# Three chained matrix products in seven block products: y over the whole contraction, with a stored third matrix of seven forms

## The chip, the cores and the metric

One NeuronCore of a Trainium2 chip. The metric is device time in microseconds of one execution. Engines: TensorE (PE; its weight loads PEld), VectorE (DVE), ScalarE (ACT), GpSimd (POOL) and SyncE (SP), which only issues DMAs. Each engine works through its own instructions in order.

## The reference, cut to what matters

Attention (4 batches, 12 heads, 448 positions, head width 64, with a mix over heads ahead of the softmax and one behind it) gives x of 1792 tokens x 768. Then

```
a = x @ w1;  b = x @ w2            # 768 -> 1024
h = a * b @ w3                     # 1024 -> 1024
x2 = h @ w_out                     # 1024 -> 768, called y in the kernel
h2 = max(x2 @ w_in, 0);  out = h2 * h2 @ w_out2     # 768 -> 2048 -> 768
```

All in float32. There is nothing between w3 and w_out, so the kernel multiplies these two once (p34, 1024 x 768) and computes y = (a * b) @ p34.

## The kernel before, in words

A float32 matrix is split into a high part (a copy rounded by ACT) and a low part (the rest, subtracted by DVE or POOL), and a product is three matmuls: high x high, high x low, low x high (`mm3`). The 1792 tokens are two halves of 896, a half is two tiles t of 448 columns. Matrices are kept transposed: a chunk is 128 rows of features x 448 tokens.

After the attention the work is a list of units, and each unit a few pieces of weights. One piece after another, `stage` issues for each engine, in an order fixed in the code: loads for the piece seven ahead (SP), the high part four ahead (ACT, `high`, L122), the low part three ahead (POOL, `rest`, L164), then functions that earlier pieces left in `late`, then the piece's own matmuls and reads (`go`). In this document a slot is the time of one piece.

Units in order, for the first half: l1 (a and b for 8 row blocks of 128), with w_out's pieces between them; p34 (8 units, 3 pieces each: w3 and w_out to p34, stored by ACT in `w34d`); the l1 units of row blocks 6 and 7; ly (y, 6 units); l3 products (named qh00 to qh07 in the trace, 7 block products of two halves each, from four products of halves of x2 and w_in); l4. During p34 and ly, `side` packs w_in for later (ACT fold L95, DVE L1116 and L1117, store). For the second half: l1 as block products (q00 to q31), ly, l3 and l4 as block products.

ly before: unit n is the block of 128 rows n of y; in 3 pieces of 3, 3 and 2 chunks of the contraction, for t = 0 and 1, PE multiplies with ab of this half. ab is stored split: `l1` and `l1_quad` multiply a and b in the PSUM bank (L789, L922), and `split_late` then makes the high (ACT, L771) and low part (DVE, L772). When a block is done, `yquad` reads it. The l3 product that follows wants seven forms of y: with B11, B12, B21, B22 for (half of the rows, t), B11, T1 = B12 - B11, T2 = B22 - T1, B22, T3 = B22 - B12, B21 and T4 = B21 - T2, each as high and low. `yquad` works per pair of row blocks j, as the blocks come.

`wl` and `wh` are ten buffers each, weight pieces of `ly` come into four `raw` buffers. PSUM has eight banks (`m`).

Of the kernel before, what the change touches and what calls it, by code (L numbers as in the profile page):

```python
# [9 lines left out]
F = mybir.dt.float32  # L10
# [28 lines left out]
def fused_kernel(ctx, tc, q, k, v, w_pre, w_post, w1, w2, w3t, wo, win, wo2, eye, out):  # L39
# [15 lines left out]
    def f32(ap):  # L55
        return ap.bitcast(F)
# [10 lines left out]
    class Weights:  # L67
# [480 lines left out]


    class Moe:  # L550
        def __init__(self, pre):
# [4 lines left out]
            self.sides, self.step = {}, 0  # L556
            self.hq = {}
            for hf in range(2):
                if hf == 0:
                    l1 = [self.l1(hf, m, s) for m in range(6) for s in range(2)]  # L560
                else:
                    l1 = [self.l1_quad(j, s) for j in range(4) for s in range(2)]
                if hf == 0:

                    wop = [self.wo_piece(c, h) for c in range(8) for h in range(2)]
                    mixed, rest = l1[:4] + wop[:6], wop[6:]
                    for i in range(8):
                        mixed.append(l1[4 + i])
                        for _ in range(1 + (i % 4 == 3)):
# [9 lines left out]
                self.units += [self.ly(hf, n) for n in range(6)]  # L579
                if hf == 0:  # L580
                    k = self.turned
                    self.free = {(i, t) for i in (*range(self.p34_at, k - 4), *range(k, k + 4)) for t in (0, 1)}
                    self.free |= {(i, 1) for i in range(k - 4, k)}
                    self.free |= {(k + 9 + e, 0) for e in range(6)}
                    self.free |= {(k + 17, 0)}
# [12 lines left out]
            for u in range(self.turned, len(self.units)):  # L598
                n, quad = len(self.units[u][0]), self.pieces[self.at[u]][0] is None
                for i in range(n if quad else 0):  # L600
                    self.lead[self.at[u] + i] = (4 if i < 6 else 3 if i < 8 else i > 9) if n > 7 else 2 if u > self.turned + 6 else 1
            self.keep = {
                self.at[i] + j: u[0][:, u[1] * j : u[1] * j + u[1]]
                for i, u in enumerate(kept) if u for j in range(len(self.units[i][0]))
            }

        def place(self, wp):
# [98 lines left out]
        def run(self, ps):  # L706
# [71 lines left out]
        def l1(self, hf, m, second):  # L778
            def run(ws, t, acc=None):
# [129 lines left out]
        def l1_quad(self, j, second):  # L909
            def done(r, t, acc, x=None, y=None):  # L910
                m = 2 * j + r
                if not second:
# [5 lines left out]
                    return  # L918
                ab = self.xy["ab", 1, m, t] = self.pair(f"ab1_{m}_{t}")
                if y is not None:  # L920
                    self.add(acc, x, y)
                nc.vector.tensor_tensor(acc, acc, self.xy["a", m, t], ALU.mult)  # L922
                self.split_late(ab, acc)

            src = [w12d[int(second), 2 * j + r] for r in range(2)]
            return self.quad(f"{j}{int(second)}", src, lambda: self.xq, 3, done)
# [88 lines left out]

        def yquad(self, hf, n, t, acc):
            j, kh = divmod(n, 2)
            if n == 0 and t == hf:
                xy = [self.new_xy(f"y{hf}_{t}", t) for t in range(2)]
                self.yq = {}  # L1020
                for c in range(3):
                    for name, u, o in (("B11", 0, 0), ("B21", 0, 3), ("T1", 1, 0), ("B22", 1, 3)):
                        self.yq[name, c] = tuple(x[:, o + c] for x in xy[u])
                    for name in ("T2", "T3", "T4"):
                        self.yq[name, c] = self.pair(f"y{hf}{name}{c}")
            b = self.yq
            V, G = nc.vector, nc.gpsimd

            def raw(name):
                b[name, j, "raw"] = self.tile(f"y{hf}{name}raw{j}")  # L1030
                return b[name, j, "raw"]

            def lo(name, x, eng=V):
                h, l = b[name, j]
                eng.tensor_tensor(l, x, f32(h), ALU.subtract)

            def hi(name, x):
                nc.scalar.activation(b[name, j][0], x, AF.Copy)

            def diff(name, x, y):  # L1040
                V.tensor_tensor(raw(name), x, y, ALU.subtract)

            name = f"B{kh + 1}{t + 1}"
            r = lambda n: b[n, j, "raw"]
            if name == "B22":
                diff("T2", acc, r("T1"))
                diff("T3", acc, r("B12"))
                hi("T2", r("T2"))
                hi("B22", acc)
                lo("T2", r("T2"))  # L1050
                lo("B22", acc)

                def rest():
                    for x in ("T3", "T4"):
                        hi(x, r(x))
                    for x in ("T3", "T4"):
                        lo(x, r(x), G if j < 2 else V)

                self.late[0].append(lambda: diff("T4", r("B21"), r("T2")))
                self.late[1].append(rest)  # L1060
                return
            nc.scalar.activation(raw(name), acc, AF.Copy)
            if name != "B12":
                hi(name, r(name))
                lo(name, r(name), G)
            if kh == 0 and all((n, j, "raw") in b for n in ("B11", "B12")):
                diff("T1", r("B12"), r("B11"))
                hi("T1", r("T1"))
                lo("T1", r("T1"), G)

        def wo_piece(self, c, h):
# [3 lines left out]
        def p34(self, m):  # L1075
            acc = {}

            def run(ws, i):
                for t in range(2):
# [4 lines left out]
                    if i < 2:  # L1084
                        continue
                    o = self.tile(f"o34_{m}_{t}")[:, :HC]
                    nc.scalar.activation(o, acc[t], AF.Copy)
                    nc.scalar.dma_start(
                        w34d[3 * t : 3 * t + 3, :, m].rearrange("n p c -> p n c"), o.rearrange("p (n c) -> p n c", c=128)
                    )  # L1090

            return [(w3t[m, :, HC * i : min(HC * i + HC, 1024)], True) for i in range(3)], run

        def ly(self, hf, n):
            acc = {}

            def run(ws, i):
                for t in (1, 0) if hf and n == 0 else (0, 1):
                    if i == 0:
                        acc[t] = self.psum(f"y{hf}_{n}_{t}")  # L1100
                    cs = range(3 * i, min(3 * i + 3, 8))
                    mm3(acc[t], [(self.chunk(ws, c), self.xy["ab", hf, c, t]) for c in cs], i == 0, i == 2)
                    if i == 2:
                        self.yquad(hf, n, t, acc[t])

            src = w34d[n].rearrange("p c n -> p (c n)")
            return [(src[:, HC * i : min(HC * i + HC, 1024)], False) for i in range(3)], run

# [215 lines left out]
```

## Time and profile before

| | us |
|---|---|
| median of 3 runs (1263.72 to 1266.94) | 1265.95 |
| the profiled execution, its own time | 1266.82 |
| its span, first to last instruction | 1265.0 |
| PE, DVE, ACT, POOL busy | 1238.2, 912.4, 776.7, 601.3 |

The page's parts are shares over the whole span. The chain of waits goes back from the last instruction: PE has 86% of it. The table of the queues gives q1 (SP's) 49.1% of 16 DMA engines and q10 (ACT's) 5.2%. What a change in one stage is worth is read from the rows of that stage.

### The profile page before, as it was taken

How to read it: one execution, taken by the hardware profiler on the slowest of the kernel's cores; microseconds unless marked ns; L12 is line 12 of the kernel's file. 1: busy time of each engine (PE TensorE's matmuls, PEld its weight loads, DVE VectorE, ACT ScalarE, POOL GpSimd, SP SyncE). 2: the span in 40 equal slices, each digit the busy share in tenths (PEclk: the TensorE clock that was granted, in tenths of full speed). 3: DMA queues.
4: the chain of work that ended last, by engine and by line, in shares of the span. 5: the costliest groups of instructions: out<-in, count | busy, mean ns of one | idle time of the engine just before them, and what ended most of it. 6: DMA issues, size and time to landing. Idle time of an engine off the chain costs nothing.

```text
span 1265.0 us, 24184 instructions
## 1 busy us (share of the span) xinstructions
PE 1238.2 (98%) x8326; PEld 1069.9 (85%) x8326; DVE 912.4 (72%) x1746; ACT 776.7 (61%) x1786; POOL 601.3 (48%) x707
## 2 busy tenths in 40 slices
PE   7999999999999899999999999999999999999998
PEld 3677777776776698999999999999999999999998
DVE  4888889889887967766455767579767424766967
ACT  5988888888987755555444756455433344653543
POOL 4354346246321313333356544444765464846756
PEclk9999999999999999999999999999999999999999
DMA  6666466565646657799654676466521116145042
GB/s 216 172 176 201 133 192 221 135 172 177 204 127 209 207 151 230 219 295 335 198 177 140 201 244 200 169 223 212 183 70 51 56 57 194 51 137 176 30 152 88
DMA packets 135696, 214.47 MB, mean 170 GB/s; under 512 B 24981, under 2 KB 104341, under 8 KB 135061
## 3 DMA queue, kind: packets, MB, share of 16 engines
q1 hardware_dynamic: 111696, 190.29, 49.1%
q10 hardware_dynamic: 23877, 22.63, 5.2%
q8 instruction: 66, 1.08, 0.4%
q14 instruction: 57, 0.47, 0.1%
HBM read 128.73 MB, written 45.61 MB: 138 GB/s over the span
## 4 chain that ended last, share of the span: by engine, by line
PE 86%; DVE 4%; DMA 3%; ACT 3%; issue 2%; POOL 2%; SPq 0%; ACTq 0%; POOLq 0%; DVEq 0%
PE l L62 16%; PE y L62 9%; PE sp L338 8%; PE tp L403 5%; PE p L62 5%; PE pv L455 5%; PE sc L312 4%; DMA r<-s 2%; PE e L62 1%; DVE pl L394 1%; DMA kraw<-k 1%; ACT p L352 1%; DVE nm L344 1%; ACT ph L378 1%; DVE p L417 1%
## 5 line engine op out<-in xcount | busy, mean ns | idle before, releaser
L164 POOL TENSOR_TENSOR wl<-f,wh 128x256 fp32r<-128x256 f32 (+1 forms) x104 | 96.9, 932 | 189.3 <-ACT wh L122 149.9
L338 PE MATMUL sp<-r,kpre 120*120 120x448 f32 x360 | 158.8, 561 | 11.6 <-ACT p L352 6.7
L352 ACT ACTIVATE p<-sp,nm 120x448 f32<-120x448 f32 x180 | 113.9, 644 | 49.9 <-DVE nm L344 49.3
L344 DVE TENSOR_REDUCE nm<-sp 120x1 f32<-120x448 f32 x180 | 107.4, 617 | 42.2 <-PE sp L338 37.9
L394 DVE SCALAR_TENSOR_TENSOR pl<-p,sm,ph 120x448 f16<-120x448 f32 (+3 forms) x270 | 131.8, 541 | 0.3 <-POOL ph L380 0.3
L367 POOL TENSOR_SCALAR sm<-sm 120x2 f32<-120x2 f32 (+3 forms) x94 | 24.5, 261 | 214.8 <-ACT p L352 210.7
L403 PEld LDWEIGHTS <-ph 120*128 120x128 f16 x1260 | 93.0, 98 | 29.8 <-issue 23.1
L378 ACT ACTIVATE ph<-p,sm 120x448 f16<-120x448 f32 (+1 forms) x180 | 107.9, 666 | 12.8 <-DVE sm L372 11.7
L403 PE MATMUL tp<-kwh,ph 120*128 120x120 f16 x630 | 106.0, 217 | 3.0 <-ACT p L415 2.1
L338 PEld LDWEIGHTS sp<-r,kpre 120*120 120x120 f32 x360 | 58.5, 183 | 55.8 <-issue 19.3
L403 PE MATMUL tp<-kwh,pl 120*128 120x120 f16 x630 | 105.1, 216 | 0.0
L403 PE MATMUL tp<-kwl,ph 120*128 120x120 f16 x630 | 105.1, 216 | 0.0
L312 PE MATMUL sc<-kt,qh 128*110 128x448 f32 (+1 forms) x192 | 98.3, 512 | 2.2 <-DVE kt L276 1.5
L323 ACT ACTIVATE s<-sc 110x448 f32<-110x448 f32 (+1 forms) x186 | 90.8, 562 | 6.3 <-PE sc L312 5.3
L122 ACT ACTIVATE wh<-f 128x256 fp32r<-128x256 f32 (+1 forms) x104 | 48.1, 463 | 57.5 <-DVE f L108 50.5
L164 POOL TENSOR_TENSOR wl<-quadh,wh 128x384 fp32r<-128x384 f32 x48 | 51.4, 1075 | 66.9 <-ACT wh L122 54.5
L455 PE MATMUL pv<-p,v 128*64 128x110 f32 (+1 forms) x1536 | 81.0, 262 | 0.6 <-ACT xs L465 0.6
L95 ACT ACTIVATE y<-raw 128x384 f32<-128x384 f32 (+1 forms) x120 | 59.0, 494 | 30.3 <-DMA raw<-wo 16.5
L455 PEld LDWEIGHTS pv<-p,v 128*64 128x64 f32 x1536 | 74.1, 137 | 4.1 <-ACT xs L465 0.9
L108 DVE SCALAR_TENSOR_TENSOR f<-raw,f 128x384 int32<-128x384 int32 (+1 forms) x120 | 71.9, 599 | 4.1
L417 DVE TENSOR_SCALAR p<-tp,iv 128x360 f32<-128x360 f32 x132 | 72.6, 577 | 2.1 <-PE tp L403 2.1
L312 PE MATMUL sc<-kt,ql 128*110 128x448 f32 (+1 forms) x192 | 70.8, 369 | 0.0
(3094 smaller groups left out, 3907.7 us busy)
## 6 DMA issues: line engine op xcount, KB each, us to landing
r<-s SPq DMA_DIRECT2D x172, 210.0 KB
raw<-w SPq DMA_DIRECT2D x32, 384.0 KB
sraw<-win SPq DMA_DIRECT2D x32, 384.0 KB
raw<-wo SPq DMA_DIRECT2D x48, 256.0 KB
kraw<-k SPq DMA_DIRECT2D x24, 448.0 KB
quadh<-wind SPq DMA_DIRECT2D x24, 384.0 KB
qraw<-q SPq DMA_DIRECT2D x35, 220.0 KB
v<-v SPq DMA_DIRECT2D x4, 1536.0 KB
```

The costliest lines, as they stand in the source:

```text
L62: nc.tensor.matmul(acc, w, x, start=(first and i == 0 and j == 0), stop=(last and i == n - 1 and j == 2), skip_group_check=again,)
L164: eng.tensor_tensor(self.out[i][1], self.ft.pop(i), f32(self.out[i][0]), ALU.subtract)
L312: nc.tensor.matmul(sc[:ic], t[:, hh * ic : hh * ic + ic], self.kt[b, h // 2][:, h % 2], start=(i == 0), stop=(i == 1))
L323: nc.scalar.activation(self.st[n][:ic, h], self.sc.pop((n, h))[:ic], AF.Copy)
L338: nc.tensor.matmul(t[:kk], self.kpre[:kk, :kk], self.rt.pop(g)[:kk], start=True, stop=True)
L344: nc.vector.tensor_reduce(nm[:kk], self.sp[g][:kk], AX.X, ALU.max, negate=True)
L352: nc.scalar.activation(p[:kk], self.sp.pop(g)[:kk], AF.Exp, bias=self.nm.pop(g)[:kk], accum_out=self.sm[g // 2][:kk, g % 2 : g % 2 + 1],)
L378: nc.scalar.activation(h[:, to], p[:, fr], AF.Copy, scale=sm)
L394: nc.vector.scalar_tensor_tensor(l[:, to], p[:, fr], sm, h[:, to], ALU.mult, ALU.subtract)
L403: nc.tensor.matmul(t[:, j], p[:, at : at + 128], w, start=(i == 0), stop=(i == 2))
L417: nc.vector.tensor_scalar(d, t[:, main], self.iv, None, ALU.mult)
L455: nc.tensor.matmul(t[64 * e : 64 * e + 64, x, :w], self.v[b][:, j, g], self.p2[n][:, j * NH + g, :w], start=(j == 0), stop=(j == JC - 1),)
```

## The change

The seven block products that l1 and l3 already use are now used for y as well, over the whole contraction: ab is cut into two halves of the rows (contraction) and two tiles, y likewise, p34 into four blocks.

- p34 is stored as seven forms of 512 x 384, `w7d[7, 4, 128, 384]`: three blocks as they come (ACT's DMA queue) and four sums or differences, made by DVE one slot later and stored by SP two slots later.
- ly has 7 units, one for each product, of 4 pieces (chunks c). In a piece, PE multiplies the 384 columns of the weight form with one chunk of the ab form: three pairs p of 128 columns, in three PSUM banks, nine matmuls. Products of even number add up in banks X, those of odd number in Z, and a bank is read four slots after it was begun or continued (`yread`).
- ab is kept unrounded in SBUF. The seven forms of it are made per chunk: a difference on DVE for T1 to T4, the high part on ACT, the low part on DVE (even c) or POOL (odd c). `plan_forms` fixes the slots: difference 12 (first half) or 14 (second), high 10 and low 9 pieces ahead, or as soon as the inputs are there.
- `yread` copies or adds the banks and makes the same seven forms of y, all of them in the last three units.
- Pieces of `ly` come into the six `quad` buffers. The side work runs in p34 and in all l1 units of row blocks 6 and 7, and in one slot of each of the first four ly units. The order of w_in's rows is the plain one.

```diff
-    w34d = dram.tile([6, 128, 8, 128], F, name="w34d")
+    w7d = dram.tile([7, 4, 128, DM // 2], F, name="w7d")
...
-                t = self.pre.tile([128, WT], F, tag="raw", name=f"raw{i}", bufs=self.nraw)
+                t = self.ap.tile([128, PW], F, tag="quad", name=f"raw{i}", bufs=6)
...
+    LY_FORMS = ("B11", "T1", "T2", "B22", "T3", "B21", "T4")
+    FORM_OF = {"T1": ("B12", "B11"), "T2": ("B22", "T1"), "T3": ("B22", "B12"), "T4": ("B21", "T2")}
+    LEAD0, LEAD1 = (12, 10, 9), (14, 10, 9)
...
-                    self.free = {(i, t) for i in (*range(self.p34_at, k - 4), *range(k, k + 4)) for t in (0, 1)}
-                    self.free |= {(i, 1) for i in range(k - 4, k)}
+                    self.free = {(i, t) for i in range(self.p34_at, k) for t in (0, 1)}
+                    self.free |= {(i, 1) for i in range(k, k + 4)}
...
+            lead = (LEAD0, LEAD1)[hf]
+            for s, n in enumerate(LY_FORMS):
+                for c in range(4):
+                    u = 4 * s + c
+                    if n[0] == "T":
+                        p = max([at(u - lead[0])] + [ready[x, c] for x in FORM_OF[n]])
+                        ready[n, c] = put(p, self.form_diff, n, c) + 1
+                    p = put(max(at(u - lead[1]), ready[n, c]), self.form_hi, n, c)
+                    p = put(max(at(u - lead[2]), p + 1), self.form_lo, n, c)
...
+        def form_hi(self, hf, n, c):
+            self.fp[hf, n, c] = self.pair(f"ab{hf}{n}{c}")
+            nc.scalar.activation(self.fp[hf, n, c][0], self.raws[hf, n, c], AF.Copy)
+
+        def form_lo(self, hf, n, c):
+            h, l = self.fp[hf, n, c]
+            (nc.gpsimd if c % 2 else nc.vector).tensor_tensor(l, self.raws[hf, n, c], f32(h), ALU.subtract)
...
                 def go():
+                    for f, *a in self.todo.pop(p, []):
+                        f(*a)
...
-                    ab = self.xy["ab", hf, m, t] = self.pair(f"ab{hf}_{m}_{t}")
-                    nc.vector.tensor_tensor(acc, acc, self.xy["a", m, t], ALU.mult)
-                    self.split_late(ab, acc)
+                    ab = self.raws[hf, f"B{m // 4 + 1}{t + 1}", m % 4] = self.tile(f"ab{hf}_{m}_{t}")
+                    nc.vector.tensor_tensor(ab, acc, self.xy["a", m, t], ALU.mult)
...
+                if m < 4:
+                    V.tensor_tensor(new(4), self.po[m, 0], acc[1], ALU.subtract)
+                else:
+                    s1, s2, s4 = (new(x) for x in (1, 2, 3))
+                    V.tensor_tensor(s1, acc[1], self.po[c, 1], ALU.add)
+                    V.tensor_tensor(s2, s1, self.po[c, 0], ALU.subtract)
+                    V.tensor_tensor(s4, acc[0], s2, ALU.subtract)
...
+                for p in range(3):
+                    if (bk, p) not in self.yb:
+                        self.yb[bk, p] = self.psum(f"y{hf}{bk}{p}")
+                    mm3(
+                        self.yb[bk, p], [(self.chunk([ws[c]], p), self.fp[hf, xn, c])],
+                        s in (0, 1, 5) and c == 0, c == 3, s not in (0, 1, 5),
                     )
+                    if c == 3:
+                        self.yread(hf, s, p, self.yb[bk, p])
...
+            if s < 3:
+                nc.scalar.activation(raw(("P1", "P5", "U2")[s]), acc, AF.Copy)
+            elif s == 3:
+                o = r["B12", p] = r["U2", p]
+                self.add(o, acc, o)
+            elif s == 4:
+                o = r["B22", p] = r["P5", p]
+                self.add(o, acc, o)
+                at(p, diff, "T3", "B22", "B12", p)
+                at(p, hi, "B22", p)
+                at(p, hi, "T3", p)
+                at(p + 1, lo, "B22", p, G)
+                at(p + 1, lo, "T3", p, G)
+                at(p + 1, lambda: self.add(raw("W"), r["P1", p], r["T3", p]))
+            elif s == 5:
+                o = r["T2", p] = r["W", p]
+                self.add(o, acc, o)
+                hi("T2", p)
+                o = r["B11", p] = r["P1", p]
+                self.add(o, acc, o)
+                hi("B11", p)
+                at(0, lo, "T2", p)
+                at(0, lo, "B11", p, G)
+                at(1, diff, "T1", "B12", "B11", p)
+                at(1, hi, "T1", p)
+                at(2, lo, "T1", p)
+            else:
+                r["B21", p] = acc
+                hi("B21", p)
+                lo("B21", p)
+                at(0, diff, "T4", "B21", "T2", p)
+                at(0, hi, "T4", p)
+                at(1, lo, "T4", p, G)
```

In `yread`, `lo` is DVE's unless G (POOL) is named, `at(k, ...)` leaves a function for the k-th slot after the next.

## Rows read from the trace of the kernel before

**Rows 1.** The page's first part; mean granted clock of the core.

```profile
PE 1238.2 (98%) x8326; PEld 1069.9 (85%) x8326; DVE 912.4 (72%) x1746; ACT 776.7 (61%) x1786; POOL 601.3 (48%) x707
core 0: 1265.0 us, clock 0.998
```

**Rows 2.** Chain of waits in order of time: start us, us, what.

```profile
598.61 28.80 PE l L62 x144
627.41 57.60 PE y L62 x288
685.01 1.80 PE qh00A L62 x9
...
1002.26 57.60 PE y L62 x288
```

**Rows 3.** Busy time (count) of each engine by stretch, clock, DMA share, GB/s.

```profile
core 0: us, PE busy (x) PEld busy (x) DVE busy (x) ACT busy (x) POOL busy (x), PEclk, DMA share, GB/s
627.40:685.00 57.60, 57.60 (x290) 53.99 (x289) 29.34 (x36) 25.53 (x52) 31.52 (x28) 1.00 0.49 163
1002.30:1059.90 57.60, 57.60 (x289) 53.99 (x288) 13.79 (x19) 21.53 (x44) 28.80 (x28) 1.00 0.35 111
685.00:706.00 21.00, 21.00 (x107) 19.47 (x106) 18.39 (x26) 13.13 (x30) 14.88 (x13) 1.00 0.43 152
```

**Rows 4.** The same view for p34 and the l1 units behind it.

```profile
532.00:598.60 66.60, 66.60 (x386) 66.60 (x385) 45.40 (x82) 36.00 (x79) 24.44 (x25) 1.00 0.94 303
598.60:627.40 28.80, 28.80 (x146) 27.00 (x145) 13.00 (x20) 12.55 (x27) 11.69 (x11) 1.00 0.67 217
```

**Rows 5.** ACT by line and shape: busy us, mean ns, idle before.

```profile
L122 ACT ACTIVATE wh<-raw 128x384 fp32r<-128x384 f32 x24 | 12.3, 515 | 5.3 <-DVE side L1117 5.3
L1038 ACT ACTIVATE y_0h<-y1B11raw 128x448 fp32r<-128x448 f32 x3 | 1.7, 580 | 0.1
L1062 ACT ACTIVATE y0B21raw<-y 128x448 f32<-128x448 f32 x3 | 1.6, 546 | 9.6 <-PE y L62 9.6
```

**Rows 6.** POOL's lows by line: ns min/median/max, first and last start.

```profile
L164 POOL TENSOR_TENSOR wl<-quadh,wh x32: 1007/1022/1402, 678.9 to 1106.9; 128x384 fp32r<-128x384 f32 x32
L1035 POOL TENSOR_TENSOR y_1l<-y0T1raw,y_1h x3: 1151/1157/1158, 639.4 to 677.8; 128x448 fp32r<-128x448 f32 x3
L1035 POOL TENSOR_TENSOR y0T31l<-y0T3raw,y0T31h x1: 1541/1541/1541, 669.3 to 669.3; 128x448 fp32r<-128x448 f32 x1
```

**Rows 7.** POOL in order of time: start us, us.

```profile
685.08 1.17 POOL L1035 TENSOR_TENSOR y_0l<-y0B21raw,y_0h 128x448 fp32r<-128x448 f32 x1 [3.20 <-PE y L62]
686.20 1.02 POOL L164 TENSOR_TENSOR wl<-quadh,wh 128x384 fp32r<-128x384 f32 x1
687.27 1.31 POOL L164 TENSOR_TENSOR wl<-Sh,wh 128x384 fp32r<-128x384 f32 x1
688.54 1.40 POOL L164 TENSOR_TENSOR wl<-quadh,wh 128x384 fp32r<-128x384 f32 x1
...
692.27 1.33 POOL L164 TENSOR_TENSOR wl<-quadh,wh 128x384 fp32r<-128x384 f32 x1
...
702.70 1.02 POOL L164 TENSOR_TENSOR wl<-Sh,wh 128x384 fp32r<-128x384 f32 x1
703.68 1.33 POOL L164 TENSOR_TENSOR wl<-quadh,wh 128x384 fp32r<-128x384 f32 x1
```

**Rows 8.** DVE by line: ns min/median/max, first and last start.

```profile
L1035 DVE TENSOR_TENSOR y_1l<-y,y_1h x6: 611/611/611, 649.2 to 1062.5; 128x448 fp32r<-128x448 f32 x6
L1035 DVE TENSOR_TENSOR y0T21l<-y0T2raw,y0T21h x1: 1377/1377/1377, 667.1 to 667.1; 128x448 fp32r<-128x448 f32 x1
L1035 DVE TENSOR_TENSOR y0T32l<-y0T3raw,y0T32h x1: 612/612/612, 690.3 to 690.3; 128x448 fp32r<-128x448 f32 x1
L1117 DVE SCALAR_TENSOR_TENSOR side<-sraw,side x32: 558/976/1396, 543.3 to 750.5; 128x384 int32<-128x384 int32 x32
```

**Rows 9.** DVE in order of time: start us, us.

```profile
686.39 1.31 DVE L1035 TENSOR_TENSOR y0T22l<-y0T2raw,y0T22h 128x448 fp32r<-128x448 f32 x1 [0.18 <-ACT y0T22h L1038]
...
688.15 0.91 DVE L1041 TENSOR_TENSOR y0T4raw<-y0B21raw,y0T2raw 128x448 f32<-128x448 f32 x1
688.99 1.37 DVE L160 TENSOR_TENSOR Sh<-quadh,Sh 128x384 f32<-128x384 f32 x1
```

**Rows 10.** POOL by line and shape: busy us, mean ns, idle before.

```profile
L164 POOL TENSOR_TENSOR wl<-raw,wh 128x384 fp32r<-128x384 f32 x24 | 26.5, 1114 | 9.9 <-ACT wh L122 9.6
```

More of the change, by code (lines that the diff above doesn't have):

```diff
@@ L605, in __init__, with slot, plan_forms, at @@
             }
+            self.todo = {}
+            for hf in range(2):
+                self.plan_forms(hf)
+        def slot(self, i, t=0):
+            return 9 + sum(len(u[0]) for u in self.units[10:i]) + t
+        def plan_forms(self, hf):
+            first = self.slot(self.turned if hf else self.ahead)
+            before = (self.turned if hf else self.ahead) - 8
+            def at(v):
+                return first + (v if hf or v >= 0 else v // 2)
+            ready = {}
+            for c in range(4):
+                for n, i in (("B11", 3), ("B22", 4), ("B21", 5), ("B12", 6)):
+                    ready[n, c] = self.slot(before + 2 * c + 1, i) + 1 if hf else 0
+                    if not hf and c > 1 and n[1] == "2":
+                        ready[n, c] = first - 4 * (4 - c) + 3 + (n[2] == "2")
+            def put(p, f, *a):
+                self.todo.setdefault(p, []).append((f, hf, *a))
+                return p
+            lead = (LEAD0, LEAD1)[hf]
+            for s, n in enumerate(LY_FORMS):
+                for c in range(4):
+                    u = 4 * s + c
[4 more added lines that the diff above has]
+                    p = put(max(at(u - lead[2]), p + 1), self.form_lo, n, c)
+                    if n == "T2":
+                        ready["T2", c] = p
+                    assert p < first + u
+        def form_diff(self, hf, n, c):
+            r = self.raws
+            x, y = (r[hf, k, c] for k in FORM_OF[n])
+            old = {"T3": "B12", "T4": "T2"}.get(n)
+            o = r[hf, n, c] = r[hf, old, c] if old else self.tile(f"{n}ab{hf}_{c}")
+            nc.vector.tensor_tensor(o, x, y, ALU.subtract)
+        def form_hi(self, hf, n, c):
[4 more added lines that the diff above has]
+            (nc.gpsimd if c % 2 else nc.vector).tensor_tensor(l, self.raws[hf, n, c], f32(h), ALU.subtract)
         def place(self, wp):
@@ L1014, in forms @@
             return done
[L1016 to L1069, printed above, removed]
         def wo_piece(self, c, h):
@@ L1085, in run @@
                         continue
[L1086 removed]
+                    o = self.po[m, t] = self.tile(f"o34_{m}_{t}")[:, :HC]
                     nc.scalar.activation(o, acc[t], AF.Copy)
[L1088 to L1092 removed]
@@ L1094, in ly @@
[L1094 to L1107, printed above, removed]
+                    if m > 3 or t == 0:
+                        nc.scalar.dma_start(w7d[5 + t if m > 3 else 0, m % 4], o)
@@ new lines, in run, with sums, new, store @@
+                if i == 2:
+                    self.late[0].append(sums)
+            def sums():
+                V, c, done = nc.vector, m % 4, []
+                def new(stage):
+                    o = self.tile(f"s34_{m}_{stage}")[:, :HC]
+                    done.append((stage, o))
+                    return o
+                if m < 4:
[5 more added lines that the diff above has]
+                    V.tensor_tensor(s4, acc[0], s2, ALU.subtract)
+                def store():
+                    for stage, o in done:
+                        nc.sync.dma_start(w7d[stage, c], o)
+                self.late[1].append(store)
@@ new lines, in yread, with raw, hi, lo @@
+        def yread(self, hf, s, p, acc):
+            V, G = nc.vector, nc.gpsimd
+            if s == 0 and p == 0:
+                self.yr = {}
+            if s == 4 and p == 0:
+                xy = [self.new_xy(f"y{hf}_{t}", t) for t in range(2)]
+                self.yq = {}
+                for c in range(3):
+                    for name, u, o in (("B11", 0, 0), ("B21", 0, 3), ("T1", 1, 0), ("B22", 1, 3)):
+                        self.yq[name, c] = tuple(x[:, o + c] for x in xy[u])
+            b, r = self.yq if s > 3 else None, self.yr
+            def raw(name):
+                r[name, p] = self.tile(f"y{hf}{name}raw{p}")
+                return r[name, p]
+            def hi(name, p):
+                if (name, p) not in b:
+                    b[name, p] = self.pair(f"y{hf}{name}{p}")
+                nc.scalar.activation(b[name, p][0], r[name, p], AF.Copy)
+            def lo(name, p, eng=V):
+                h, l = b[name, p]
+                eng.tensor_tensor(l, r[name, p], f32(h), ALU.subtract)
+            def diff(name, x, y, p):
+                r[name, p] = self.tile(f"y{hf}{name}raw{p}")
+                V.tensor_tensor(r[name, p], r[x, p], r[y, p], ALU.subtract)
+            def at(k, f, *a):
+                self.late[k].append(lambda: f(*a))
+            if s < 3:
[31 more added lines that the diff above has]
+                at(1, lo, "T4", p, G)
```

31 lines of the change are left out of this document (19 added, 12 removed).

## The prediction

> **What bounds the kernel now.** First the page's engine line and the granted clock [rows 1]: PE 98% busy, clock 0.998, the others below 73%. Read next the chain of waits around the two stages that the change rewrites [rows 2]: y of the first half is 57.60 us of PE alone, 288 matmuls, and follows 28.80 us of l1 and precedes the qh products without a gap; y of the second half is again 57.60 us. Then the busy time by stretch [rows 3]: in both y stretches PE is busy 57.60 of 57.60 us, DVE 29.34 and 13.79, ACT 25.53 and 21.53, POOL 31.52 and 28.80. So from 476 us on nothing but the number of matmuls sets the time, at 57.60/288 = 0.200 us each, and POOL has the least room after PE. A change here pays 0.200 us for each matmul that it removes, and gives it back where another engine can no longer keep ahead.
>
> **What the change removes on PE.** Before, a half takes 6 blocks x 2 tiles x 8 chunks x 3 = 288 matmuls of 448 columns; after, 7 products x 4 chunks x 3 lockstep pairs x 3 = 252 of the same shape. 36 x 2 halves x 0.200 = 14.4 us less, all on the path. Had nothing else mattered, the profiled execution's 1266.82 us would become 1252.4. The l1, p34 and qh products keep their matmuls.
>
> **What it adds, and what hides it.** A y stage becomes 28 slots (one form of one chunk, nine matmuls) of 1.80 us, 50.4 us instead of 57.60.
>
> p34: twelve output tiles are stored instead of being split over 16 stores by ACT, and SP stores 16 sums: 28 stores of 192 KB instead of 16, +2.3 MB. In its 66.60 us [rows 4] DMA runs at 0.94 and 303 GB/s, which puts full share at 322 GB/s; 20.2 + 2.3 MB need 69.9 us of it, 3.3 us too many. The operands stand three to four slots ahead of PE (one slot there is 2.8 us), which covers it, and the next 28.80 us have share 0.67. I take nothing; without that cover it is 3.3 us, the other end 0. The 16 sums are DVE work of about 0.6 us each, 9.6 us on 45.40 of 66.60: hidden. SP's stores wait for these sums with the next weight loads queued behind them; they are issued two slots after the products, so SP waits no longer than DVE is late. Nothing.
>
> ACT: per half 28 form highs at 0.58, 28 weight highs at 0.515 instead of 12 of that and six narrower, nine copies (0.546) and 21 highs of y as before [rows 5]. The y stretch holds about 20 of the form highs, so 25.53 + 11.6 + 5.8 = 43 us in 50.4 with 16 ab splits gone: hidden, and PE reaches the piece only four slots later. Loads: 28 pieces of 192 KB are 5.5 MB in 50.4 us, 109 GB/s, on stretches that carried 163 and 111 GB/s including the old loads: hidden. TensorE's bank reads: X and Z are read four slots (7.2 us) before they are written again, against 0.55 us a copy: hidden as long as DVE is less than some 6 us late.
>
> POOL and DVE are the part that is not hidden. A weight low of 384 columns takes POOL 1.02 us, a 448-wide low 1.16; back to back they follow at 0.98 (702.70 to 703.68) and 1.12 us (685.08 to 686.20) [rows 6, 7]. A 448-wide DVE subtraction takes 0.611 us when one operand comes from PSUM, always; with both in SBUF it is 0.612 us beside an idle POOL and 1.31 to 1.38 beside a busy one [rows 8, 9]. And it costs POOL: 1.541 us instead of 1.157 for a low, 1.31, 1.40 and 1.33 instead of 1.02 for a weight low [rows 6, 7]. At 688.15 a DVE subtraction starts inside POOL's 687.27 one and ends 0.48 us after it; POOL's next, started 688.54, lasts 0.38 us longer. They take turns. Price of one DVE instruction with two SBUF operands to a busy POOL: 0.31 to 0.38 us, I take 0.36, since most are 448 wide. The ends for the range are 0 (they miss each other) and the instruction's whole 0.61.
>
> Now POOL's list, from the first y slot to the weight low of the first qh product, which is issued after the nine y lows of B22, T3 and B11 (the low of a piece is issued three slots ahead):
> - 26 weight lows x 0.98 = 25.5 us.
> - form lows of odd chunks: 10 in the first half, 11 in the second, and 9 y lows: 19 or 20 x 1.12 = 21.3 or 22.4.
> - DVE instructions with two SBUF operands issued meanwhile. First half: 10 form lows, 9 form differences, 12 of y (T3, W, T2's low, T1), 8 of the side work (L1116 and L1117, the latter 0.558 us alone and up to 1.396 [rows 8]) and 2 weight sums = 41. Second half: 9 + 10 + 12 = 31. Times 0.36: 14.8 and 11.2.
>
> Sums: 46.8 + 14.8 = 61.6 us, and 47.9 + 11.2 = 59.1. PE wants that weight low at 28 x 1.80 + 0.4 = 50.8 us. Late by 10.8 and 8.3 us. In the first half POOL then owes four weight lows, three lows of T4, five turns and one more weight low, 3.9 + 3.4 + 1.8 + 1.0 = 10.1 us, before the sixth product, which is 5 x 1.80 = 9.0 us later: 1.1 more. In the second half most qh weights come split from memory, so nothing is added. DVE itself is in order: the PSUM adds and the T1 and T2 parts stand behind instructions that wait for POOL, so the same lateness shows there, and I don't count it twice. That POOL also waits at times for a form's high, and that not every DVE instruction meets a POOL one, I let cancel.
>
> Total: -14.4 + 10.8 + 8.3 + 1.1 = +5.8, and 1266.82 + 5.8 = 1272.6. The profiled execution is 0.9 us above the median of the runs, 1265.95, so I write 1272.
>
> **A rule weighed.** The rows above show POOL losing 0.31 to 0.38 us to a DVE subtraction of 0.612 us [rows 6, 8]. The Trainium skill, page "SBUF — State Buffer", section "Who interferes with whom", says that a VectorE instruction with two SBUF inputs and a GpSimd instruction that reads SBUF exclude each other: the second to start is fully blocked until the first has finished. The turns of rows 7 and 9 agree with the order that it gives, but by its letter POOL would lose the whole 0.61 us; the sum would be 1291 by the rule and 1272 by the rows, and the former is the third rival below.
>
> **The rivals.**
> 1. Faster: the two engines mostly miss each other. In the 21 us after the first y [rows 3], POOL's 13 lows take 14.88 us, where 1.16 + 12 x 1.02 = 13.4 would do: 1.48 us over the 11 DVE instructions of that kind, 0.13 each. With 0.13 the lists are 52.1 and 51.9 us, late by 1.3 and 1.1, with T4 about 3 us: 1266.8 - 14.4 + 3 = 1255. It decides from 0.28 us an instruction on: there 72 x 0.28 + 46.8 + 47.9 + about 1 - 101.6 makes the 14.4 us that PE saves. For it: POOL gets ahead in the longer slots before the first y. Against it: POOL was idle 6 us in that stretch, and here its own list already fills 46.8 of 50.8.
> 2. No change, 1266: a price near 0.28, between the two; the loss equals the gain.
> 3. Far slower: each DVE instruction costs POOL its whole 0.61 us. 46.8 + 25.0 = 71.8, 47.9 + 18.9 = 66.8: late by 21 and 16, T4 by 2 more: 1291. Against it are the 1.31 to 1.541 us of rows 6 and 7, none of which shows more than 0.38.
> 4. p34's stores are not hidden and 3.3 us come on top of the forecast: 1276.
>
> **How the numbers follow.** Forecast 0.50, by itself 1268 to 1278 (price 0.31 to 0.42); rival 1 0.28, rival 2 0.14, rival 3 0.03, rival 4 0.05. 0.3% of this kernel is 3.8 us, about what a measurement can tell from none. Rival 1 gives faster 0.28; rival 2 and the lowest part of the forecast give the same, 0.19; the rest is slower, 0.53. The range runs from rival 1's time to above rival 4: 1255 to 1281; the free cover (1252) and rival 3 stay outside.
>
> **What would show it.** In the trace after: y matmuls at 252 a half and still 0.200 us apart where they run (the gain). POOL without pauses through the last third of both y stages, weight lows of 1.3 us and more than 1.15 in the mean (now 1.114 for those of y [rows 10]), and PE waiting for POOL's wl in the last y pieces and before the first qh product, first half more than second. If instead PE has no idle time between 598 and 723 us, the price of the turns was wrong, and 1252 to 1256 is the answer. PE gaps inside p34 would be rival 4. A PE that waits for forms or y operands of DVE while POOL is idle would make the mechanism wrong even at the right time.

## The result, and the profile after

The changed kernel takes 1282.75 us (median of 5 runs, 1281.57 to 1286.19) beside 1263.97 for the kernel before on the same chip: 1.015 of it, interval 1.0136 to 1.0163, so 18.8 us slower. The profiled execution took 1281.57 us with a span of 1279.8. Forecast was 1272, at most 1281: the sign held, and the mechanism in the second half; in the first half a step of it failed.

The page's first part answers to [rows 1]; the second line is the granted clock. PE has 72 matmuls less and its share fell; POOL has 46 instructions more and 72.9 us more busy time.

```profile
PE 1231.7 (96%) x8254; PEld 1056.7 (83%) x8254; DVE 999.8 (78%) x1816; ACT 796.4 (62%) x1830; POOL 674.2 (53%) x753
core 0: 1279.8 us, clock 0.997
```

Busy time by stretch, columns as in [rows 3]. The first two lines run from the first y matmul of a half to the end of the weight low that the first qh product waits for, the third is p34, the last two are the end of that low's wait and what follows it.

```profile
622.90:690.40 67.50, 54.86 (x255) 46.27 (x253) 65.23 (x66) 37.22 (x77) 61.56 (x48) 1.00 0.50 163
1013.90:1073.20 59.30, 51.81 (x255) 47.16 (x253) 51.82 (x48) 33.13 (x69) 58.13 (x46) 1.00 0.46 144
527.70:594.30 66.60, 66.60 (x386) 66.59 (x386) 48.43 (x89) 33.95 (x75) 23.73 (x24) 1.00 0.91 301
686.60:690.40 3.80, 0.16 (x1) 0.00 (x0) 3.80 (x3) 0.58 (x1) 3.80 (x4) 1.00 0.00 1
690.40:694.30 3.90, 3.86 (x11) 3.44 (x12) 3.90 (x6) 2.62 (x6) 2.32 (x2) 0.56 0.19 69
```

The stretch that PE could walk in 50.8 us takes 67.5 and 59.3. In the second half POOL is busy 58.13 of 59.30; in the first it is busy 61.56 and idle 5.94, all of this before 642.5 us, and DVE is the fuller of the two, 65.23. p34 is as full of PE as in [rows 4].

What PE waits for, first half (620 to 735 us) and then second (1000 to 1095): us in total, times, longest.

```profile
PE y0X L62 <- POOL wl L164: 5.5, 5, 2.1
PE qh00A L62 <- POOL wl L164: 3.7, 1, 3.7
PE qh00A L62 <- ACT s1h L946: 2.1, 1, 2.1
PE y0Z L62 <- POOL wl L164: 1.6, 3, 0.8
PE y0Z L62 <- ACT wh L122: 1.4, 2, 0.8
PE y0Z L62 <- ACT ab0T43h L658: 0.5, 1, 0.5
...
PE y1X L62 <- POOL wl L164: 3.9, 3, 2.2
PE qh10A L62 <- POOL wl L164: 3.7, 1, 3.7
PE q31C L62 <- DVE q31B L910: 2.1, 1, 2.1
```

What POOL waits for in the first half (620 to 692 us; one of the four waits for ACT, 1.5 us, ends with the first y matmul), and its own weight lows by line and shape from 622.9 to 690.4 and from 1012 to 1073 us, which answer to [rows 10]: 1.300 and 1.238 us in the mean where it was 1.114.

```profile
POOL wl L164 <- ACT wh L122: 5.1, 4, 1.5
POOL ab0T23l L662 <- ACT ab0T23h L658: 2.2, 1, 2.2
```

```profile
L164 POOL TENSOR_TENSOR wl<-raw,wh 128x384 fp32r<-128x384 f32 x26 | 33.5, 1300 | 5.3 <-ACT wh L122 5.1
...
L164 POOL TENSOR_TENSOR wl<-raw,wh 128x384 fp32r<-128x384 f32 x26 | 31.8, 1238 | 0.0
```

Two of these waits in order of time, ACT and then POOL. A weight high of ACT stands behind a fold of the side work whose load is late, and POOL's low behind that high; a form high waits for a difference of DVE, which ran a side step (2.0 us) and a low just before it, and POOL's form low waits for the high.

```profile
629.80 0.56 ACT L95 ACTIVATE sraw<-sraw 128x384 f32<-128x384 f32 x1 [1.70 <-DMA sraw<-win]
630.49 0.52 ACT L122 ACTIVATE wh<-raw 128x384 fp32r<-128x384 f32 x1
...
634.72 0.58 ACT L658 ACTIVATE ab0T23h<-T2ab 128x448 fp32r<-128x448 f32 x1 [2.62 <-DVE T2ab L654]
```

```profile
631.09 2.12 POOL L164 TENSOR_TENSOR wl<-raw,wh 128x384 fp32r<-128x384 f32 x2 [1.49 <-ACT wh L122]
635.38 1.14 POOL L662 TENSOR_TENSOR ab0T23l<-T2ab,ab0T23h 128x448 fp32r<-128x448 f32 x1 [2.17 <-ACT ab0T23h L658]
```

The end of the stretch, where PE stands longest, in order of time (start us, us), by POOL, then DVE, then PE. POOL's three lows of B11 take 4.49 us while DVE subtracts T2 and T1 at 1.4 to 1.57 us each; both are in SBUF, and [rows 7, 9] showed the same turns. PE stands from 686.6 to 690.44, and its next eleven matmuls follow each other at 0.30 to 0.37 us instead of 0.20.

```profile
684.56 4.49 POOL L1161 TENSOR_TENSOR y_0l<-y0P1raw,y_0h 128x448 fp32r<-128x448 f32 x3
689.02 1.37 POOL L164 TENSOR_TENSOR wl<-quadh,wh 128x384 fp32r<-128x384 f32 x1
```

```profile
685.03 1.57 DVE L1161 TENSOR_TENSOR y0T21l<-y0Wraw,y0T21h 128x448 fp32r<-128x448 f32 x1
686.52 1.55 DVE L1161 TENSOR_TENSOR y0T22l<-y0Wraw,y0T22h 128x448 fp32r<-128x448 f32 x1
687.99 4.23 DVE L1165 TENSOR_TENSOR y0T1raw<-y0U2raw,y0P1raw 128x448 f32<-128x448 f32 x3
```

```profile
690.44 0.47 PE L62 MATMUL qh00A<-y_0h,wl 128*128 128x448 f32 x1 [3.69 <-POOL wl L164]
...
691.80 0.57 PE L62 MATMUL qh00A<-y_0h,wh 128*128 128x448 f32 x1
692.17 0.57 PE L62 MATMUL qh00A<-y_0l,wh 128*128 128x448 f32 x1
...
694.54 0.36 PE L62 MATMUL qh00B<-y0T21h,wl 128*128 128x448 f32 x1
694.74 0.36 PE L62 MATMUL qh00B<-y0T22h,wh 128*128 128x448 f32 x1
```

To compare runs I use three stages, read from PE's rows. **Y0** runs from the first y matmul of the first half to the end of the third group of qh products (qh02C); **Q** is the q products; **Y1** runs from the last q matmul to the first one of qh11. Before they take 95.5, 100.8 and 70.2 us; without the 36 matmuls a half they would be 88.3, 100.8 and 63.0, the floor. After they are 109.0, 103.2 and 73.2: 20.7 + 2.4 + 10.2 = 33.3 us above the floor, 18.9 above before. The other stages differ by 0.3 at most. The spans differ by only 14.8, because p34 began at 527.5 us here and 531.9 before; between the profiled kernels it begins anywhere from 526.5 to 531.9, so single spans carry that much of attention, and the stages don't.

### The profile page after: what moved, and what is told of

It reads as the page before. It is cut to its first block, busy times and chain, and to the rows that moved or that the text cites. A ratio compares the mean times of both kernels' runs of the same rounds, so it can differ in the third digit from the quotient of the medians.

```text
span 1279.8 us, 24312 instructions
## 1 busy us (share of the span) xinstructions
PE 1231.7 (96%) x8254; PEld 1056.7 (83%) x8254; DVE 999.8 (78%) x1816; ACT 796.4 (62%) x1830; POOL 674.2 (53%) x753
## 4 chain that ended last, share of the span: by engine, by line
PE 76%; POOL 7%; DMA 5%; DVE 5%; issue 4%; ACT 2%; SPq 1%; ACTq 0%; POOLq 0%
PE l L62 14%; PE sp L338 8%; PE tp L403 6%; PE pv L455 5%; PE sc L312 4%; POOL wl L164 4%; PE p L62 3%; PE y1X L62 2%; DMA r<-s 2%; DMA kraw<-k 1%; PE y1Z L62 1%; PE e L62 1%; DVE pl L394 1%; DMA qraw<-q 1%; DVE nm L344 1%
## 5 line engine op out<-in xcount | busy, mean ns | idle before, releaser
L164 POOL TENSOR_TENSOR wl<-f,wh 128x256 fp32r<-128x256 f32 (+1 forms) x104 | 95.4, 918 | 194.9 <-ACT wh L122 161.1
L338 PE MATMUL sp<-r,kpre 120*120 120x448 f32 x360 | 158.6, 559 | 10.8 <-ACT p L352 6.5
L95 ACT ACTIVATE y<-raw 128x384 f32<-128x384 f32 (+1 forms) x120 | 59.1, 495 | 40.5 <-DMA raw<-w3t 13.9
L164 POOL TENSOR_TENSOR wl<-raw,wh 128x384 fp32r<-128x384 f32 x56 | 70.9, 1279 | 5.3 <-ACT wh L122 5.1
L108 DVE SCALAR_TENSOR_TENSOR f<-raw,f 128x384 int32<-128x384 int32 (+1 forms) x120 | 68.7, 572 | 4.1
```

The costliest lines, as they stand in the source:

```text
L164: eng.tensor_tensor(self.out[i][1], self.ft.pop(i), f32(self.out[i][0]), ALU.subtract)
L338: nc.tensor.matmul(t[:kk], self.kpre[:kk, :kk], self.rt.pop(g)[:kk], start=True, stop=True)
```

## The experiments

Fourteen runs. A ratio is to the kernel before on the same chip, with its interval; runs without one were executed once, and these I read by stages, since a single span also carries what attention varies by. Line numbers are those of each run's own kernel. Stages in us:

| run | median us | ratio | Y0 | Q | Y1 |
|---|---|---|---|---|---|
| before | 1263.97 | | 95.5 | 100.8 | 70.2 |
| after | 1282.75 | 1.015 | 109.0 | 103.2 | 73.2 |
| e1_side_away | 1292.46 | 1.0223 (1.0203 to 1.0243) | 104.8 | 104.6 | 71.8 |
| e2_no_pool_form_lows | 1265.11 | | 99.8 | 101.5 | 68.9 |
| e3_no_dve_form_lows | 1275.90 | | 109.0 | 100.9 | 69.2 |
| e4_no_weight_lows | 1264.31 | | 97.0 | 102.0 | 67.6 |
| f1_defer_lows | 1282.66 | 1.0145 (1.013 to 1.016) | 110.6 | 104.5 | 70.5 |
| f2_side_in_p34 | 1293.04 | 1.0235 (1.0211 to 1.0259) | 107.0 | 103.6 | 73.3 |
| f3_keep_weight_lows | 1277.11 | 1.0098 (1.0082 to 1.0114) | 111.4 | 102.1 | 67.6 |
| f4_all_three | 1291.10 | 1.0208 (1.0187 to 1.0228) | 110.2 | 102.1 | 69.0 |
| g1_late_t4 | 1275.92 | 1.0098 (1.0081 to 1.0115) | 109.6 | 102.2 | 66.2 |
| g2_no_side_dve | 1281.22 | | 103.8 | 103.2 | 73.2 |
| g3_ahead | 1282.57 | 1.0155 (1.0138 to 1.0172) | 118.4 | 102.2 | 66.2 |
| g4_dve_form_lows | 1280.37 | | 109.8 | 102.6 | 70.4 |
| h1_both_away | 1260.55 | | 95.9 | 102.0 | 63.7 |
| h2_side_early | 1275.95 | 1.0093 (1.0076 to 1.011) | 104.7 | 102.1 | 66.2 |

**Work taken away: whose time is it?** The weight lows (e4):

```diff
...
                     if not self.pieces[i][1]:
                         w.high(i)
+                        w.out[i] = (w.out[i][0],) * 2
+                        w.ft.pop(i)
```

> POOL's lows of the 28 weight pieces of each y stage are left out (the high part in their place). Theory P: 26 us of POOL's list gone in each half, all waits for wl gone, and with them the end waits and the slow matmuls: 20 us or more faster, 1256 to 1263; what is left in the first half are waits for ACT behind the side work, 2 to 4 us, and the second half's wait before q31C. Rival (DVE or ACT ends last): under 8 us, 1275 or more.

Measured: 12.0 us less in Y0, 5.6 in Y1. In the first half PE's remaining waits are at the seam of y and qh:

```profile
PE qh00A L62 <- ACT s1h L948: 3.0, 1, 3.0
PE qh00A L62 <- POOL wl L164: 1.9, 1, 1.9
```

The form lows of odd chunks, on POOL (e2), and of even chunks, on DVE (e3; the test is then for 0; the high part takes the low's place):

```diff
...
             h, l = self.fp[hf, n, c]
+            if c % 2 == 1:
+                return
```

> POOL's lows of the ab forms (odd chunks, 14 a half) are left out; PE multiplies with the high part in their place, so its work is the same. Theory P (POOL's list with its turns with DVE ends last): some 10 x 1.12 us less of list in each y stage, against 8 us of waits at the end of each and 2 us of slower matmuls behind them: both go, about 16 to 22 us faster than the changed kernel, 1261 to 1267, and POOL no longer 14.4 of 14.4 us busy in the last third. Rival (ACT's or DVE's order ends last, POOL only waits for it): under 5 us, 1278 or more.

> DVE's lows of the ab forms (even chunks, 14 a half) are left out in the same manner; POOL keeps all of its work. Theory P with turns at 0.36 us: 10 turns less in each half, 3.6 us each, and DVE's order gets free of 10 x 1.4 us: 7 to 12 us faster, 1271 to 1276. Rival 1 (POOL's own instructions alone fill its time and turns cost it nothing): under 3 us, 1280. Rival 2 (DVE's order ends last): as much as without POOL's lows, 1262 to 1267.

Measured: e2 takes 9.2 us less in Y0 and 4.3 in Y1, though the waits for the first qh product's low stay (3.3 and 3.7 us). e3 takes nothing from POOL, yet Y1 falls by 4.0 and Q by 2.3: 4.0 for ten DVE instructions is 0.40 each, paid by POOL, and q31's wait for DVE is gone. Y0 does not move, so the total came out as forecast by another sum. There the first qh product's low comes 3 us earlier against the first y matmul (64.3 us, not 67.5), but the wait for the bank read of s1 is then 4.0 us instead of 2.1, and PE runs longer at the lower clock (second line; granted 0.82 over these 16 us, and 0.73 over the 8 us ahead of them):

```profile
PE qh00A L62 <- ACT s1h L952: 4.0, 1, 4.0
```

```profile
684.00:700.00 16.00, 9.95 (x38) 8.24 (x37) 15.96 (x18) 7.69 (x16) 13.02 (x11) 0.82 0.21 74
```

DVE's side instructions in and just ahead of y (g2):

```diff
+            if 14 <= k - 2 < 26:
+                f = self.sides[k - 2] = self.tile(f"side{k - 2}")[:, :HC]
+                nc.scalar.activation(f, self.w.raw["side", k - 2][:, :, 1].bitcast(F), AF.Copy)
-            if 0 <= k - 2 < 32:
+            elif 0 <= k - 2 < 32:
```

> Left out: the two DVE instructions of side steps 14 to 25, that is, part of the w_in product is not computed (ACT does one plain copy in their place); the steps' DMAs stay. If the many small waits of PE in the first 35 us of y of the first half (7.6 us) come from DVE's side instructions in front of its own forms and from their turns with POOL, these waits fall by 4 to 7 us and the first half's stage goes from 109 to 102 to 105 us. If they come from the side's loads landing late (ACT's weight highs stand behind a side copy that waits for a DMA), they stay, and the stage is 107 to 109 us.

Measured: Y0 5.2 us less, Y1 the same. So the side work makes that part. Whether it does so by DVE's time or by the loads is not separated: the loads are still there, but each waits for a buffer that DVE's second instruction gave back and that ACT's copy now gives back, and ACT's waits for side loads in the y stretch, 3.3 us in two, are gone too. From the first y matmul to the low of the first qh product POOL has no idle time left, and that stretch is 62.0 us where it was 67.5:

```profile
627.20:689.20 62.00, 54.64 (x255) 47.86 (x253) 53.57 (x51) 35.62 (x74) 62.00 (x48) 0.97 0.48 158
```

Both (h1: the edits of e4 and g2, and T4's highs at step 2 instead of 0):

> Left out: POOL's weight lows of y's forms (the high stands in their place) and DVE's two instructions of side steps 14 to 25; and T4's highs come two steps later in ACT's list. If POOL's list and the shared turns are the whole loss, both stages reach what PE's matmuls alone need, 88.3 and 63.0 us, within 2 us: about 1252 to 1256. If ACT's form highs, its order or the loads hold the stages too, they stay at 94 to 97 and 66 to 68 us: 1262 to 1265.

Measured: Y1 at 63.7, its floor within 0.7; Y0 at 95.9, 7.6 above. So in the second half POOL's list with its turns and the place of T4's highs are all but 0.7 us of the loss: without the weight lows alone (e4) Y1 was 67.6, with PE waiting 2.1 us for s1. In the first, something remains at the seam: DVE is busy 14.37 of the 14.40 us from 665.6 (POOL 11.95), on the T3, W, T1 and T2 work of y and on six sums of the qh weights (L160, 6.7 us from 663 to 692), where the second half has four narrower ones of 2.7 us and loads the rest.

**All the work kept, its place or order changed.** Eight side steps of l1 and y into l4 behind them (e1), or into a third slot of each p34 unit (f2, shown):

```diff
-                    self.free = {(i, t) for i in range(self.p34_at, k) for t in (0, 1)}
-                    self.free |= {(i, 1) for i in range(k, k + 4)}
+                    self.free = {(i, t) for i in range(self.p34_at, k - 4) for t in (0, 1, 2)}
+                    self.free |= {(i, 1) for i in range(k - 4, k)}
```

> The side work leaves the ly slots and half of the l1 slots before them, for l4 of the first half. In the changed kernel PE loses 7.6 us in the first y stage before its last product, where ACT's weight highs stand behind side folds that wait for sraw loads, and DVE runs 24 side instructions there. Theory S (the side work makes these early waits): they go, and the later ones shrink a little, 6 to 10 us faster than the changed kernel, about 1275. Rival P (POOL's and DVE's list for the forms makes them): 8 fewer DVE instructions with two SBUF operands at 0.36 us, 3 us, about 1280. Neither expects a change in the second half.

> The side work leaves the ly slots and half of the l1 slots, for the third slot of each p34 unit; nothing after the first half's y changes. In the run with the side work moved to l4 the first y stage with its three qh products took 104.8 us instead of 109.0 but l4 and later stages lost more. Theory S: 4 to 6 us of the first y stage go and nothing is lost elsewhere, 1277 to 1279. Rival M (p34's DMA share, 0.86 to 1.02 in the changed kernel, is full): PE waits in p34 or in l1 for weights, 3 to 8 us, and the total is the same or slower.

Measured: e1 came to neither of its totals, f2 to that of rival M. e1 takes 4.2 us from Y0 and loses 4.4 in l4 and 9.7 from there to the first q product, where PE now waits for weights and sums at a clock of 0.88 (757 to 800 us). f2 takes 2.0 from Y0, and PE waits in p34 and l1 instead, where the DMA share is 0.90 and 0.92 (0.91 and 0.88 in the changed kernel) in stages that last longer; y starts 105.5 us after p34, not 95.4.

```profile
PE p L62 <- POOL wl L164: 2.0, 3, 0.7
PE p L62 <- ACT wh L122: 1.9, 2, 1.0
PE l L62 <- ACT wh L122: 1.2, 1, 1.2
PE l L62 <- POOL wl L164: 1.0, 3, 0.4
```

The lows of T3 and B22 later in POOL's order (f1):

```diff
-                at(p + 1, lo, "B22", p, G)
-                at(p + 1, lo, "T3", p, G)
+                at(6, lo, "T3", p, G)
+                at(8 + p, lo, "B22", p, G)
```

> Only the order of POOL's y lows is changed: T3's three move from slots 21 to 23 to slot 26 and B22's from 21 to 23 to 28 to 30, behind the lows of B11 and of the first qh weights; nothing is left out. Theory P (POOL's list up to the first qh product ends last): that list gets shorter by six lows and their turns, 7 to 9 us, and the waits for wl of the last y product and the first qh product, 8.2 and 8.7 us with 2 us of slower matmuls behind each, mostly go: 5 to 8 us in each half, 1267 to 1273. Rival D (DVE's list ends last, POOL only follows it in turns): under 2 us a half, 1279 or more, and PE then waits for T1, T2 or ACT's reads in place of wl.

Measured: no change in time; Y1 gains 2.7 us, and Y0 and Q lose 1.6 and 1.3. In the first half the low of the first qh product is there 61.1 us after the first y matmul, not 67.5, and the wait for it shrinks from 3.7 to 1.9 us, but PE waits 5.0 instead of 2.1 for s1, which ACT reads behind T4's highs:

```profile
PE qh00A L62 <- ACT s1h L946: 5.0, 1, 5.0
PE qh00A L62 <- POOL wl L164: 1.9, 1, 1.9
```

The weight lows of the first half stored, and loaded in the second, where POOL then makes none (f3), and this with f1 and f2 (f4):

```diff
+                if i in self.lyp and not self.lyp[i][0]:
+                    nc.sync.dma_start(w7s[self.lyp[i][1], self.lyp[i][2]], f32(w.out[i][1]))
...
+                if i in self.lyp and self.lyp[i][0]:
+                    w.place(i, width=HC)
+                    nc.sync.dma_start(f32(w.out[i][1]), w7s[self.lyp[i][1], self.lyp[i][2]])
```

> The lows of the 28 weight pieces made in the first half are stored and loaded in the second, where POOL then makes none (ACT still makes the highs). Theory P: the second y stage (from the last q product to the second qh pair) goes from 73.2 to about 67.6 us, as in the run without weight lows, and with the wait before q31C some 6 to 7 us are won, 1276; the first half stays as it is. Rival M (5.5 MB more of stores in a stretch with DMA share 0.5 to 0.67): loads come late in the first half, up to 5 us back. Rival D (DVE's list ends last): under 2 us.

> All three together, with the whole computation. Theory P and S: first y stage from 109.0 to about 93 us (88.3 would be without any wait), second from 73.2 to 65 (63.0 without a wait), q without its 2.4: about 26 us faster than the changed kernel, 1254 to 1260, and so faster than the kernel before. If DVE's list ends last, 1268 or more.

Measured: f3 takes 5.6 us from Y1, as e4 did without the work; Y0 gets 2.4 longer. f4 pays for the side work in p34 again.

f3 and f1 together, with T4's highs behind the bank read of s1 (g1), and with the first half's weights and forms begun earlier (g3: also LEAD0 18, 16, 15 and a lead of 4 for y's weights):

```diff
-                at(0, hi, "T4", p)
-                at(1, lo, "T4", p, G)
+                at(2, hi, "T4", p)
+                at(3, lo, "T4", p, G)
```

> Three edits: the weight lows of the first half are written to memory and loaded back in the second, so POOL makes none of them there; the lows of T3 and B22 come later in POOL's list; T4's highs come two steps later in ACT's list, behind the bank read that the s1 sum of the first qh product waits for (now they stand before it and wait for DVE). If the POOL list and the order of the last ACT instructions are together what holds the end of y, the second half's stage falls from 73.2 to about 64 or 65 us, the first half's from 109 to about 105 (its POOL list is as long as before): about 1268 to 1272. If the s1 wait only follows POOL's, the second half stays at 67 to 70 and the time is 1275 to 1278. If the T4 products then wait for their late highs, nothing is gained over 1277.

> The three edits of the run before, and the weights of the first half's y loaded and split earlier: POOL begins on them during l1, where it has idle time. If POOL's list is what holds the first half, each weight low made ahead of y takes 1.0 us from the 109 us stage: with eight or nine ahead it is about 97 to 100 us, and the time 1262 to 1266. If the waits there are the side work's (DMA, ACT), the stage stays above 104 us: 1268 to 1272. If the earlier loads collide with l1's, l1 gets longer than 28.8 us and the time is above 1272.

Measured: g1's total is that of its second case. Its Y1 is 66.2, 4.0 us below that of the kernel before: where the weight lows are not made, the change pays. Its Y0 is 109.6 all the same. The low of the first qh product is there 61.6 us after the first y matmul, not 67.5, but what comes later is as late as ever, now in front of many small waits:

```profile
PE qh00A L63 <- POOL wl L165: 1.9, 1, 1.9
PE qh00A L63 <- ACT s1h L961: 1.8, 1, 1.8
...
PE qh00B L63 <- DVE u2h L925: 1.6, 1, 1.6
...
PE qh00C L63 <- ACT wh L123: 1.0, 1, 1.0
PE qh00D L63 <- POOL y0T40l L1176: 0.9, 1, 0.9
```

g3 missed: ACT's first copy of a bank of y now stands behind highs of forms that were moved ahead of it and wait for DVE, and PE waits 5.9 us for that copy:

```profile
645.39 0.58 ACT L665 ACTIVATE ab0T33h<-ab 128x448 fp32r<-128x448 f32 x1 [1.81 <-DVE ab L661]
645.88 1.40 ACT L1188 ACTIVATE y0P1raw<-y0X 128x448 f32<-128x448 f32 x3
```

All form lows on DVE (g4), and eight side steps ahead of p34 with all of g1 (h2):

```diff
-            (nc.gpsimd if c % 2 else nc.vector).tensor_tensor(l, self.raws[hf, n, c], f32(h), ALU.subtract)
+            nc.vector.tensor_tensor(l, self.raws[hf, n, c], f32(h), ALU.subtract)
```

> All lows of the ab forms on DVE instead of every other one on POOL (20 or 21 more DVE instructions of two SBUF operands, 21 POOL lows of 1.12 us less). POOL's list per half falls by 11.2 to 12.3 us and rises by ten turns, 3.6 to 4.0 us: net 7.6 us less. If POOL's list alone sets the end of y, each stage falls by some 7 us and the time is about 1268 to 1270. If POOL and DVE share one path, which is full, DVE's low of 0.61 us holds it for less time than POOL's, and the gain is about the same; but if DVE's own list is what is full (14.33 of 14.40 us busy there), PE waits for forms and PSUM sums instead, and the time is 1283 or more.

> All work is done. The second half's weight lows come from memory, T3's, B22's and T4's splits come later (the run g1), and of the side work eight steps go from l1 and y of the first half to the l1 products ahead of p34, where DVE is busy 33 of 52 us and DMA has share 0.71: y has no side step of its own, l1 has half of them. If the amount of DVE work beside POOL's list sets the first half, it falls from 109.6 us by 3 to 6 and the time is 1270 to 1273. If the place makes no difference because POOL's list alone is long enough, it stays at 1276. If eight more steps are too much for the DMA engines in that stretch, PE waits there or in p34 and the time is above 1277.

Measured: g4 gains 2.8 in Y1 and nothing in Y0, so neither of its two cases holds throughout. In its first half POOL is idle 21.0 us, and the low of the first qh product is still there only after 66.1: POOL waits 19.4 us for ACT's weight highs, ACT as long for DVE's differences and sums, and DVE is busy 63.88 us. So DVE's list seems to take the place of POOL's there; that is read from this trace alone.

```profile
624.30:690.40 66.10, 55.02 (x255) 48.04 (x253) 63.88 (x77) 36.42 (x76) 45.07 (x37) 0.97 0.50 164
```

h2 takes 4.9 us from Y0 against g1, as its first case said, but p34 and l1 take 2.0 more between them (an l1 matmul waits 0.6 us for a low). Its profiled execution is 2.7 us faster than that of g1, the medians show no difference: 1275.95 and 1275.92.

## Why the prediction was wrong

The signs named for the mechanism are in the trace: weight lows above 1.15 us in the mean, POOL without pauses in the last third of both y stages, PE waiting for POOL's wl in the last y pieces and before the first qh product. Point by point, with the lists taken from the profile after:

- **PE's saving.** Held: 252 matmuls a half, 0.200 us apart where they run, 14.4 us.
- **p34 and its stores, SP, the sums.** Held: PE has no idle time from 527.7 to 622.9 us. Rival 4 is out.
- **POOL's list, second half.** Forecast 59.1 us and 8.3 late. Measured 59.3 (POOL busy 58.13), 8.5 late: 0.70 + 1.27 + 2.38 before T4's weight lows and 3.86 before the first qh product, 8.2 us. The parts agree too: POOL's own work is 46.9 us (forecast 47.9), the turns 11.2 (11.2), its idle time 1.2 (nothing).
- **POOL's list, first half.** Forecast 61.6 us and 10.8 late. POOL is busy 61.56 us, and that agreement is luck: 27 weight lows and 20 lows are 48.9 us of its own work, 2.1 more than counted, and the turns are 12.7 us, 2.1 less, although 52 DVE instructions of the counted kinds ran beside it and not 41 (14 of the side work, not 8). The list ends after 67.5 us, 16.7 late. The step that failed is "That POOL also waits at times for a form's high, and that not every DVE instruction meets a POOL one, I let cancel": POOL is idle 5.94 us in that stretch, and nothing cancelled it. It waits for ACT's weight highs and one form high, which stand behind side loads and behind DVE's side work; g2 takes DVE's side instructions away, and POOL has no idle time and the list ends at 62.0. With idle time in it, a list longer than the stretch cannot catch up, so early waits of PE (7.6 us up to 667) are not made good later.
- **The price of a turn.** Forecast 0.36, and it held. POOL's busy time above its own in the second half (25 weight lows at 0.98 and 20 lows at 1.12 make 46.9) is 58.13 - 46.9 = 11.2 us over 34 DVE instructions with two SBUF operands, 0.33 each; in g2's first half, where POOL is never idle, it is 62.00 - 48.9 = 13.1 us over 37, 0.35; e3 gives 0.40. In the first half, with POOL's idle time, it is 12.7 us over 52, 0.24. The rule of the Trainium skill, page "SBUF — State Buffer", section "Who interferes with whom", would have it 0.61. The direction agrees and the size does not: rival 3's price is out, and so is rival 1's 0.13.
- **What follows the list.** Forecast 1.1 us in the first half and nothing in the second. Measured 2.36 for the bank read of s1 and 1.70 at the lower clock in the first, 1.7 in the second. ACT reads s1 after T4's highs, and these wait for DVE, which I had not put in any list; f1 shows that this chain takes the place of POOL's when POOL is earlier. "I don't count it twice" was wrong there: DVE's order is a second bound, right behind POOL's.
- **Q.** Forecast nothing. Measured 2.4 us: DVE's form work of the second half, which starts in q, delays q31B, and PE waits 2.1 us (the last of the waits shown above). Without DVE's form lows (e3) Q is 100.9.

Sum: 16.7 + 4.1 + 8.5 + 1.7 + 2.4 - 14.4 = 19.0 us, against 18.9 by the stages. Of the 13 us that the forecast's +5.8 lacks, 5.9 are POOL's idle time in the first half, 3.0 what follows there, 1.7 the clock in the second half, 2.4 q.

What stays open: the 7.6 us that h1 leaves in the first half. DVE is full there, and the six weight sums are the difference to the second half that I found, but no run took them away. Also open is how the side work's share in POOL's idle time divides between DVE's time and the loads. No kernel here that does all the work is faster than the one before; f3, g1 and h2 are the nearest, at 1.01.

## What to carry to other kernels

When a change moves work from the bound to engines that have room "on average", write each engine's list for the stretch and add the time it will stand idle for its inputs: a list that is longer than its stretch never gets that back. Plan two engines that take turns like these as one: reordering, or handing work from one to the other, made a stage up to 4.9 us shorter, and other stages or waits took all or part of it back; the largest gain with all work kept came from work not done twice (weight lows loaded instead of made, 5.6 us in the second half). And look for the second list: when the first was relieved, a bank read behind late highs, or DVE's list, took its place.

## What the hardware showed

A wait of PE can cost more than its length. After 3.85 us without a matmul, itself after a stretch with PE busy 3.41 of 6.00 us, the next matmuls came 0.30 to 0.37 us apart; the granted clock was 0.56 over 3.9 us, mostly the lower of its two levels, 1.2 GHz, and the 1.7 us lost come on top of the wait. The Trainium skill, page "TensorE: Matmul & The Clock Gate", Part 1, describes such a fall to half rate when PE idles, and the trace agrees. I had counted waits alone. A shorter wait, 2.08 us at 699.4 us, cost only 0.1 us more than its length. In e3 the waits before the seam are fewer, but the lower clock lasts longer, which is part of why its Y0 does not gain.
